# Slot stores and gathers tied to matmuls, and the experts' second layer kept two chunks behind

## The chip, the cores and the metric

The kernel runs on one core of one Trainium2 chip. The metric is the device time of one execution in microseconds (us), median of several runs. The engines are named as in the profile: PE is TensorE (matmuls), PEld its weight loads, DVE is VectorE, ACT is ScalarE, POOL is GpSimd, SP is SyncE, which here only issues DMAs. POOLq and the like are the engines' sequencers. "Idle before, releaser" is the time an engine stood idle before an instruction and what ended that; "issue" means that nothing which the profile shows was waited for.

## The reference, cut to what matters

2048 tokens of width 448 pass through two branches, and a gate per token mixes them:

```python
g = _sigmoid((x * gate_w).sum(-1, keepdims=True))
a = _A_ref(x, A_wqkv, A_w_phi, A_wo)      # linear attention, 16 heads of 28
b = _B_ref(x, B_w_gate, B_w1, B_w2)       # 8 experts, top 2 per token
return g * a + (1 - g) * b
```

Branch A: q, k, v from `x @ wqkv`; per head a 28x28 map, then two softmaxes (of the map and of its negative) joined to 56 features; `kv` is the sum over all tokens of features times v; each query's features are multiplied by it and normalised; then `@ wo`. Branch B: for each expert e, `h = silu(xf @ w1[e]) @ w2[e]` with 448 to 1792 to 448, weighted by the softmax over the two best logits, and zero for the other six experts.

## The kernel before, in words

Sums are made in pairs of a rounded high part and its remainder (`XH`, `XL` and so on), so one product is two or three matmuls; `kpairs` lists eleven pairs for a product over 448, and `mm3` issues them.

**Query, key and value tiles.** 16 tiles of 128 tokens. A first loop over them makes keys, values, logits and the running `kv` state. A second loop, `for t in range(NT + 2)`, is the one that the change touches first. Step t has, in the order of the program: `raise_` (exp on ScalarE, tile t + 3), `lower` (row maxima on VectorE, L562, and their subtraction on GpSimd, L563, tile t + 4), `attend(t)` (64 matmuls of 64x64 into two PSUM banks, L859) and `weigh(t)` (six VectorE operations, then an add and a copy on GpSimd that make `om`, L880 and L882), `project(t - 2)` (eleven matmuls, `ao`) with its output row stored by SP, `flip(t + 2)` (eight transposes, `et`), `turn(t - 1)` (four transposes of `om`, `ot`, L889), for the first nine steps `ask(t + 7)` (eleven matmuls), and then the GpSimd DMAs below.

**Routing.** `route` works out for each token its two experts, their weights and its slot in each expert's list, in two groups of eight tiles, a piece per step (`advance`). For each tile and choice one record per token is then written to a table in DRAM by an indirect DMA that GpSimd issues: `store(n)` takes the next n of the 32 (L455). Sixteen of them go in the first loop, between the loops and in step 0, sixteen in steps 2 to 6 (`STORES` gives the numbers that differ from 3). When all are issued, `table()` has SP read the lists back (sixteen small DMAs, L911), `rows(0, 1)` makes row numbers for expert 0 on GpSimd (L915, L919), `gather(0, c)` fetches the rows of chunk c of expert 0's tokens, 128 at a time (L768, five of them, two per step), `rows(1, E)` makes the other experts' numbers, and `first_tokens` turns the rows.

**Experts.** Experts are handled by size; the first has 552 places, the next two 544, the others 488 to 504. The hidden layer of 1792 is cut into 16 chunks (`fc`) of 128. Per chunk `first(e, fc, hf)` makes the first layer (`hp`, L115, in two pieces for the three large experts), silu on ScalarE (`hs`, L961) and its high and low part on VectorE (`hx`, L967 and L970). `second(e, fc)` adds the second layer into `acc` (L1021). Chunks whose first layer is issued wait in `held`; `keep` says how many may. Weights come two chunks at a time by SP (`wr`) and are split by ScalarE and VectorE (`halve`). At chunks 4 to 8 of expert e the rows of expert e + 1 are asked for, four indirect DMAs of 128 rows of 512 bytes per chunk of tokens (L772); at chunks 9 to 13 `tokens` has ScalarE copy (L783) and VectorE turn them. `leave(e)` weights the sums and adds them to the output by indirect DMAs of GpSimd (L934).

**What sets the order.** In both loops the order of TensorE, ScalarE and VectorE is that of the program. GpSimd and SP are ordered by a planner, but `in_turn` ties GpSimd's instructions of the loops to each other in the order of the program. `after(i, others)` makes an instruction wait for others by a semaphore, `follow` only keeps the order on one engine. The experts' gathers have no `in_turn`; they go as soon as one of the five `xg` buffers is free.

Of the kernel before, what the change touches and what calls it, by code (L numbers as in the profile page):

```python
# [18 lines left out]
P = 128  # L19
# [31 lines left out]
QASKS = {t: t + 7 for t in range(9)}  # L51
PEND = 0
ROWS = 1
SPLIT = 13
STORES = {3: 4, 4: 4, 5: 4, 6: 4}
VAHEAD = 6
AHEAD = 2
WARM = 2
# [16 lines left out]
def gated_mix(ctx: ExitStack, tc: tile.TileContext, xt, xq, wk, wq, wv, wphi, wo, w12, out):  # L75
# [13 lines left out]
    def after(i, others):  # L89
        for o in others:  # L90
            tc.add_manual_dep(i.ins, o.ins.name, mybir.DependencyInfo(mybir.DependencyClass.Sync,
                                                                      mybir.DependencyReason.DATA),
                              reason="what no_dep between its peers leaves out")

    def follow(i, o):
        tc.add_manual_dep(i.ins, o.ins.name, mybir.DependencyInfo(mybir.DependencyClass.NoSync,
                                                                  mybir.DependencyReason.SCHED_ONLY),
                          reason="what is needed sooner goes first")
# [4 lines left out]
    def in_turn(i, kind=None):  # L103
        if runs["on"]:
            if kind is None or kind != runs["kind"]:
                runs.update(before=runs["last"], last=[], kind=kind)
            for o in runs["before"]:
                follow(i, o)
            runs["last"].append(i)
        return i  # L110

    def mm3(o, pairs):
        n = len(pairs)
        for i, (a, b) in enumerate(pairs):
            nc.tensor.matmul(o, a, b, start=i == 0, stop=i == n - 1)  # L115

    def split(hi, lo, src, hi_engine="act"):
        if hi_engine == "act":
# [331 lines left out]
        nc.vector.tensor_copy(slot_i, slot_f)  # L450
        stores.extend((slot_i[:, t, k:k + 1], rec[:, ts.start + t, k, :]) for t in range(n) for k in range(2))

    def store(n):
        for at, what in stores[:n]:
            i = in_turn(nc.gpsimd.indirect_dma_start(  # L455
                out=tabd[:, :], out_offset=bass.IndirectOffsetOnAxis(ap=at, axis=0), in_=what, in_offset=None), "slots")
            after(i, filled)
            for o in sc:
                tc.declare_no_dep(i.ins, o.ins, reason="slots of their own")
            sc.append(i)  # L460
        del stores[:n]
# [87 lines left out]
    def signed(e):  # L549
        return e[:, :, 0:56].rearrange("p h (s d) -> p h s d", s=2)  # L550
# [5 lines left out]
        nc.scalar.activation(e4[:, :, 1], src, AF.Copy, scale=-1.0)  # L556


    def lower(e, n, pool):
        e4 = signed(e)  # L560
        mx = pool.tile([P, H, 2], F32, tag="mx", name=f"mx{n}", bufs=2)
        nc.vector.tensor_reduce(out=mx, in_=e4, axis=AX.X, op=ALU.max)  # L562
        in_turn(nc.gpsimd.tensor_tensor(out=e4, in0=e4, in1=mx.unsqueeze(3).to_broadcast([P, H, 2, DH]),  # L563
                                        op=ALU.subtract))


    def key(t):
# [178 lines left out]
    def extra(e):  # L746
        return EXS[e] if e < LARGE else 0
# [9 lines left out]
        return 4 if narrow(e) else 2  # L757


    def gather(e, c):  # L760
        if c == nm and not extra(e):
            return
        n = 4 if c < nm else -(-extra(e) // 32)
        t = pm.tile([P, 4, P], F32, tag="xg", name=f"xg{e}{c}", bufs=nm + 1)
        xg[e, c] = t
        if e == 0:
            ids, m = (idm[:, e * nm + c:e * nm + c + 1], P) if c < nm else (idx[:, e:e + 1], EX)
            in_turn(nc.gpsimd.indirect_dma_start(out=t[0:m].rearrange("p a k -> p (a k)"), out_offset=None, in_=x_rows,  # L768
                                                 in_offset=bass.IndirectOffsetOnAxis(ap=ids, axis=0)))
            return  # L770
        for b in range(n):
            i = nc.gpsimd.indirect_dma_start(  # L772
                out=t[:, b], out_offset=None, in_=xq,
                in_offset=bass.IndirectOffsetOnAxis(ap=idq[:, e, 4 * c + b:4 * c + b + 1], axis=0))
            if e == 1:
                for o in runs["last"]:
                    follow(i, o)


    def low_parts(pool, t, name, eng=nc.vector):  # L780
# [73 lines left out]
    def attend(t):  # L854
        n_ = two_banks(f"n{t}").rearrange("p (a j) (b d) -> p a (j b) d", a=2, b=2)
        for j in range(NJ):
            for a, h in enumerate(half):
                for b in half:
                    nc.tensor.matmul(n_[b, a, j, 0:60], et[t][h, j, b], B[h, j], start=True, stop=True)  # L859
        return n_.rearrange("p a j d -> p (a j) d")  # L860

    def weigh(t, n_):
# [39 lines left out]
    def table():  # L902
        for r in range(E):
            v = nc.values_load(byrank[0:1, r:r + 1], engines=SPONLY, min_val=0, max_val=E - 1)
            todo = [(tabm[:, r * nm:(r + 1) * nm], tabd[bass.ds(v * OWN, MAIN), :], P)]
            if r < LARGE:
                n = extra(r)
                for h in range(copies(r)):
                    todo.append((tabx[h * n:(h + 1) * n, r:r + 1], tabd[bass.ds(v * OWN + MAIN, n), :], n))
            for dst, src, p in todo:  # L910
                i = nc.sync.dma_start(dst, src.rearrange("(c p) two -> p c two", p=p))  # L911
                after(i, sc)
# [159 lines left out]
    for t in range(NT + 2):  # L1072
        u = t + QAHEAD
        if t - 1 in QASKS:
            signs(EQ[QASKS[t - 1]], pq[QASKS[t - 1]])
        elif t == 0:
            signs(EQ[6], pq[6])
        if 1 <= t and u - 1 < NT:
            raise_(u - 1)
        advance(QSTEPS.get(t, 2))  # L1080
        if u < NT and t < LOWER:
            lower(EQ[u], f"q{u}", pr)
        if t < NT:
            weigh(t, attend(t))
        if u < NT and t >= LOWER:
            lower(EQ[u], f"q{u}", pr)
        if t >= 2:
            if t == NT + 1:
                fill_in()
            leave_row(t - 2, project(t - 2))  # L1090
        if t + 2 < NT:
            flip(t + 2)
        if t == NT:
            fill_in()
        if 1 <= t <= NT:
            turn(t - 1)
        if t in QASKS:
            ask(QASKS[t], some=(0 if t else 5, 11))
        if t == NT - 1:
            fill_in()  # L1100
        if t == PEND:
            pe_stack.close()
            pm = ctx.enter_context(tc.tile_pool(name="pm", bufs=2, side="right", reuse_waits="tile"))
            pw = ctx.enter_context(tc.tile_pool(name="pw", bufs=1, side="right", reuse_waits="tile"))
            ph = ctx.enter_context(tc.tile_pool(name="ph", bufs=2, side="right", reuse_waits="tile"))
        store(STORES.get(t, 3))
        if at is None and not routes:
            routes.append(ranks())
            at = NT
        if at == NT and not stores and not routes:  # L1110
            table()
            at = t
        k = t - (NT if at is None else at)
        if k == ROWS:
            rows(0, 1)
        if k == ROWS + 3:
            rows(1, E)
        if ROWS <= k < ROWS + 3:
            for c in range(2 * (k - ROWS), min(2 * (k - ROWS) + 2, nm + 1)):
                gather(0, c)  # L1120
        if k == 2:
            load(0)
            splits += [halve(0, 1), halve(0, 2)]
        part_way()
        if ROWS + 2 <= k < ROWS + 3 + nm:
            g = first_tokens(k - ROWS - 2)
            next(g)
            coming.append(g)
        if SPLIT <= t < SPLIT + 3 and splits:
            if next(splits[0], 0) == 0:  # L1130
                del splits[0]
                if splits:
                    next(splits[0])
# [11 lines left out]
    for s in range(E * NFC):  # L1145
        e, fc = divmod(s, NFC)
        k, i = divmod(s, 2)
        token = tokens(e + 1, fc - 9) if e + 1 < E and 9 <= fc <= 9 + nm else iter(())
        next(token, 0)
        if i == 0 and k + 2 < E * NFC // 2:  # L1150
            load(k + 2)
        if k + 1 < E * NFC // 2:
            for _ in halve(k + 1, 1 + i):
                pass
        next(token, 0)
        if e + 1 < E and 4 <= fc <= 4 + nm:
            gather(e + 1, fc - 4)
        for hf in range(pieces(e)):
            if (e, fc, hf) not in fill:
                first(e, fc, hf)  # L1160
        held.append((e, fc))
        advance(1)
        if e == E - 1 and fc > NFC - LATE:
            continue

        keep = 1 if e == 0 or fc == 0 or fc >= 7 else 2
        while len(held) > keep:
            h = held.pop(0)
            second(*h)
            if h[1] == NFC - 1:  # L1170
                leave(h[0], order(h[0]))
                if h[0] == E - 2:
                    settle()
# [102 lines left out]
```

## Time and profile before

| what | value |
|---|---|
| median of 3 runs (lowest to highest) | 833.13 us (832.22 to 835.84) |
| the profiled execution: own time, span | 834.39 us, 832.7 us |
| mean granted TensorE clock | 0.988 |
| busy: PE, DVE, POOL, ACT | 804.8, 480.2, 342.4, 317.3 us |
| experts' gathers L772 | 114, 120.6 us of POOL |
| slot stores L455 | 32, 31.5 us of POOL |
| DMA, mean | 103 GB/s |

The second loop begins at about 117 us of the span and the experts' first chunk at about 228 us. In rows of instructions the columns are start, duration, engine, line, operation, output and inputs, count, and in brackets the idle time before it with its releaser. In rows of waits they are the total in us, the number of times, and the longest.

### The profile page before, as it was taken

The page shows a single profiled execution, that of the slowest core. Times are in us where ns is not written, and L with a number is a line of the kernel's source. Part 1 is how long each engine was busy: PE and PEld are TensorE (multiplying, and loading weights), DVE is VectorE, ACT ScalarE, POOL GpSimd, SP SyncE. Part 2 cuts the span into 40 slices and gives each one's busy share as a digit, 9 for nine tenths or more (in the row PEclk, how much of TensorE's full clock was granted, in tenths as well). Part 3 has the DMA queues.
Part 4 walks back from the last instruction along what each step waited for, and adds up shares of the span by engine and source line. Part 5 has one row for each costly group of instructions (what it writes and reads, how often), then busy time and mean ns, then how long its engine had stood idle before and what let it go on. Part 6 is the DMA issues. An engine that isn't in the chain of part 4 may idle for free. (4 is left out here: it accounts for less than half of the span.)

```text
span 832.7 us, 14729 instructions
## 1 busy us (share of the span) xinstructions
PE 804.8 (97%) x5672; PEld 712.7 (86%) x5672; DVE 480.2 (58%) x1048; ACT 317.3 (38%) x553; POOL 342.4 (41%) x344
## 2 busy tenths in 40 slices
PE   9999999899999899999999999999989999999996
PEld 6988887778999789998999888888878888888885
DVE  4597976456775567456645554654555465375431
ACT  5543454345642334333333342342433334244221
POOL 6666876665406256026614350730531143003003
PEclk9999998999999899999999999999999999999999
DMA  8420000015143226423733362463345237225303
GB/s 231 134 81 2 1 3 24 24 39 172 56 164 136 67 88 170 129 73 125 168 90 122 117 148 98 140 148 107 112 125 133 99 125 185 95 94 134 101 1 44
DMA packets 38910, 85.45 MB, mean 103 GB/s; under 512 B 11216, under 2 KB 19552, under 8 KB 38836
## 3 DMA queue, kind: packets, MB, share of 16 engines
q1 hardware_dynamic: 28612, 67.85, 24.6%
q0 software_dynamic: 10224, 16.61, 10.3%
q8 instruction: 46, 0.75, 0.4%
q14 instruction: 28, 0.23, 0.1%
HBM read 71.62 MB, written 12.82 MB: 101 GB/s over the span
## 5 line engine op out<-in xcount | busy, mean ns | idle before, releaser
L1021 PE MATMUL acc<-w2h,hx 128*128 128x448 f32 (+3 forms) x910 | 278.5, 367 | 3.2 <-DVE hx L967 3.1
L772 POOL DMA_INDIRECT xg<-in_xq_dram,idq x114 | 120.6, 1058 | 224.5 <-ACT xgh L799 172.0
L115 PE MATMUL hp<-xgh,w1h 128*128 128x272 f32 (+4 forms) x616 | 198.0, 336 | 5.7 <-ACT hs L961 3.1
L961 ACT ACTIVATE hs<-hp 128x272 f32<-128x272 f32 (+4 forms) x154 | 74.1, 484 | 323.7 <-issue 204.1
L115 PE MATMUL hp<-xgh,w1l 128*128 128x272 f32 (+4 forms) x616 | 196.9, 335 | 0.0
L1021 PEld LDWEIGHTS acc<-w2h,hx 128*128 128x128 f32 (+3 forms) x910 | 169.2, 186 | 26.3 <-issue 5.3
L967 DVE CAST hx<-hs 128x504 fp32r<-128x504 f32 (+5 forms) x154 | 56.2, 365 | 222.9 <-ACT hs L961 194.6
L1021 PE MATMUL acc<-w2l,hx 128*128 128x448 f32 (+1 forms) x462 | 169.4, 367 | 0.0
L115 PEld LDWEIGHTS hp<-xgh,w1h 128*128 128x128 f32 x616 | 116.3, 189 | 17.2 <-ACT hs L961 3.7
L115 PEld LDWEIGHTS hp<-xgh,w1l 128*128 128x128 f32 x616 | 116.4, 189 | 9.7
L934 POOL DMA_INDIRECT out_dram<-y,tabm x32 | 53.5, 1670 | 160.0 <-ACT y L1038 98.3
L115 PE MATMUL hp<-xgl,w1h 128*128 128x272 f32 (+4 forms) x462 | 104.4, 334 | 0.7 <-issue 0.7
L1021 PEld LDWEIGHTS acc<-w2l,hx 128*128 128x128 f32 (+1 forms) x462 | 85.9, 186 | 8.5
L970 DVE TENSOR_TENSOR hx<-hs,hx 128x276 fp32r<-128x276 f32 (+5 forms) x168 | 85.1, 514 | 5.3
L115 PEld LDWEIGHTS hp<-xgl,w1h 128*128 128x128 f32 x462 | 77.0, 189 | 8.8 <-issue 0.7
L741 DVE TENSOR_TENSOR w1l<-wr,w1h 128x1024 fp32r<-128x1024 f32 x56 | 68.0, 1215 | 3.6 <-ACT w1h L739 2.6
L741 DVE TENSOR_TENSOR w2l<-wr,w2h 128x896 fp32r<-128x896 f32 x56 | 60.3, 1076 | 11.0 <-ACT w2h L739 7.7
L739 ACT ACTIVATE w1h<-wr 128x1024 fp32r<-128x1024 f32 x56 | 58.9, 1052 | 0.0
L739 ACT ACTIVATE w2h<-wr 128x896 fp32r<-128x896 f32 x56 | 52.9, 945 | 0.0
L799 ACT ACTIVATE xgh<-xgt 128x512 fp32r<-128x512 f32 (+5 forms) x35 | 20.9, 597 | 38.1 <-DVE xgt L816 28.8
L586 POOL TENSOR_TENSOR ek<-ek,sk 128x896 f32<-128x896 f32 x16 | 27.1, 1699 | 19.0 <-DVE sk L585 9.1
L455 POOL DMA_INDIRECT tabd<-rec,slot_i x32 | 31.5, 984 | 7.6 <-issue 7.3
(221 smaller groups left out, 1020.8 us busy)
## 6 DMA issues: line engine op xcount, KB each, us to landing
wr<-in_w_dram SPq DMA_DIRECT2D x56, 512.0 KB
wr<-in_w_dram SPq DMA_DIRECT2D x56, 448.0 KB
xr<-in_xt_dram SPq DMA_DIRECT2D x15, 256.0 KB
out_dram<-aos SPq DMA_DIRECT2D x16, 224.0 KB
xg<-in_xq_dram,idq POOLq DMA_INDIRECT x114
out_dram<-zero SPq DMA_DIRECT2D x5, 224.0 KB
wraw_v<-in_wv_dram SPq DMA_DIRECT2D x4, 229.0 KB
wraw_k<-in_wk_dram SPq DMA_DIRECT2D x4, 224.0 KB
```

Source lines behind the costliest of these rows:

```text
L115: nc.tensor.matmul(o, a, b, start=i == 0, stop=i == n - 1)
L455: i = in_turn(nc.gpsimd.indirect_dma_start(out=tabd[:, :], out_offset=bass.IndirectOffsetOnAxis(ap=at, axis=0), in_=what, in_offset=None), ...
L586: in_turn(nc.gpsimd.tensor_tensor(out=by_head(e), in0=by_head(e), in1=s_.unsqueeze(2).to_broadcast([P, 2 * H, DH]), op=ALU.mult))
L739: nc.scalar.activation(h, raws[s][layer - 1], AF.Copy)
L741: nc.vector.tensor_tensor(out=l, in0=raws[s][layer - 1], in1=h.bitcast(F32), op=ALU.subtract)
L772: i = nc.gpsimd.indirect_dma_start(out=t[:, b], out_offset=None, in_=xq, in_offset=bass.IndirectOffsetOnAxis(ap=idq[:, e, 4 * c + b:4 * c ...
L799: nc.scalar.activation(xh, src, AF.Copy)
L934: return nc.gpsimd.indirect_dma_start(out=out, out_offset=bass.IndirectOffsetOnAxis(ap=idx_ap, axis=0), in_=y, in_offset=None, compute_op= ...
L961: nc.scalar.activation(hs[:, tsl], hp[:, 0:n], AF.Silu)
L967: nc.vector.tensor_copy(h[:, tsl], hs[:, tsl])
L970: nc.vector.tensor_tensor(out=h[:, a + o:b + o], in0=hs[:, a:b], in1=h[:, a:b].bitcast(F32), op=ALU.subtract)
L1021: nc.tensor.matmul(acc[e][c][:m, 0:D], l, r, start=fc == 0 and k == 0, stop=fc == NFC - 1 and k == len(pr) - 1)
```

## The change

In the second loop stores and expert 0's gathers move up to just behind `attend`, and each waits for the last matmul of `attend(t)`; the table's reading and `rows(0, 1)` move with them, and `rows(0, 1)` and the gathers of expert 0 come in the steps named below. Of `lower`, the maxima (`tops`) stay ahead of `attend`, and the subtraction (`drop`) comes behind the stores and gathers and ahead of `weigh`. The other experts' gathers become a generator that gives two DMAs per chunk from chunk 4 on, each waiting for the last matmul that `mm3` has issued, which is the last of the first layer of the chunk before. `keep` is 2 from chunk 1 to the last for experts 1 to 6, where it was 2 to chunk 6 only.

```diff
+ASKED = {1: (0, 1, 2), 2: (3, 4)}
-STORES = {3: 4, 4: 4, 5: 4, 6: 4}
+STORES = {6: 4}
...
-            nc.tensor.matmul(o, a, b, start=i == 0, stop=i == n - 1)
+            reached["pe"] = nc.tensor.matmul(o, a, b, start=i == 0, stop=i == n - 1)
...
-    def store(n):
+    def store(n, behind=()):
...
-            after(i, filled)
+            after(i, [*filled, *behind])
...
+    def gathers(e):
+        for c in range(nm + (extra(e) > 0)):
+            t = pm.tile([P, 4, P], F32, tag="xg", name=f"xg{e}{c}", bufs=nm + 1)
+            xg[e, c] = t
+            for b in range(4 if c < nm else -(-extra(e) // 32)):
+                i = nc.gpsimd.indirect_dma_start(
+                    out=t[:, b], out_offset=None, in_=xq,
+                    in_offset=bass.IndirectOffsetOnAxis(ap=idq[:, e, 4 * c + b:4 * c + b + 1], axis=0))
+                after(i, [reached["pe"]])
+                if e == 1:
+                    for o in runs["last"]:
+                        follow(i, o)
+                yield
...
-        if u < NT and t < LOWER:
-            lower(EQ[u], f"q{u}", pr)
+        early_top = u < NT and t < LOWER
+        if early_top:
+            top = tops(EQ[u], f"q{u}", pr)
         if t < NT:
-            weigh(t, attend(t))
-        if u < NT and t >= LOWER:
+            n_ = attend(t)
+        behind = [reached["n"]]
+        store(STORES.get(t, 3), behind)
+        if at is None and not routes:
+            routes.append(ranks())
+            at = NT
+        if at == NT and not stores and not routes:
+            table()
+            at = t
+        k = t - (NT if at is None else at)
+        if k == ROWS + 1:
+            rows(0, 1)
+        for c in ASKED.get(k - ROWS, ()):
+            gather(0, c, behind)
+        if early_top:
+            drop(EQ[u], top)
+        if t < NT:
+            weigh(t, n_)
+        if u < NT and not early_top:
             lower(EQ[u], f"q{u}", pr)
...
-        if k == ROWS:
-            rows(0, 1)
         if k == ROWS + 3:
             rows(1, E)
-        if ROWS <= k < ROWS + 3:
-            for c in range(2 * (k - ROWS), min(2 * (k - ROWS) + 2, nm + 1)):
-                gather(0, c)
...
-        if e + 1 < E and 4 <= fc <= 4 + nm:
-            gather(e + 1, fc - 4)
+        if e + 1 < E and fc == 4:
+            asked = gathers(e + 1)
+        if e + 1 < E and fc >= 4:
+            for _ in range(2):
+                next(asked, None)
...
-        keep = 1 if e == 0 or fc == 0 or fc >= 7 else 2
+        keep = 1 if e == 0 or fc == 0 or fc >= 7 and e == E - 1 else 2
```

More of the change, by code (lines that the diff above doesn't have):

```diff
@@ L110, in in_turn @@
         return i
+    reached = {}
     def mm3(o, pairs):
@@ L556, in signs, with tops, drop, lower @@
         nc.scalar.activation(e4[:, :, 1], src, AF.Copy, scale=-1.0)
-    def lower(e, n, pool):
+    def tops(e, n, pool):
+        mx = pool.tile([P, H, 2], F32, tag="mx", name=f"mx{n}", bufs=2)
+        nc.vector.tensor_reduce(out=mx, in_=signed(e), axis=AX.X, op=ALU.max)
+        return mx
+    def drop(e, mx):
         e4 = signed(e)
-        mx = pool.tile([P, H, 2], F32, tag="mx", name=f"mx{n}", bufs=2)
-        nc.vector.tensor_reduce(out=mx, in_=e4, axis=AX.X, op=ALU.max)
         in_turn(nc.gpsimd.tensor_tensor(out=e4, in0=e4, in1=mx.unsqueeze(3).to_broadcast([P, H, 2, DH]),
                                         op=ALU.subtract))
+    def lower(e, n, pool):
+        drop(e, tops(e, n, pool))
     def key(t):
@@ L757, in copies, with gather @@
         return 4 if narrow(e) else 2
[L760 to L763, printed above, removed]
+    def gather(e, c, behind):
         t = pm.tile([P, 4, P], F32, tag="xg", name=f"xg{e}{c}", bufs=nm + 1)
         xg[e, c] = t
[L766 to L777, printed above, removed]
+        ids, m = (idm[:, e * nm + c:e * nm + c + 1], P) if c < nm else (idx[:, e:e + 1], EX)
+        after(in_turn(nc.gpsimd.indirect_dma_start(out=t[0:m].rearrange("p a k -> p (a k)"), out_offset=None, in_=x_rows,
+                                                   in_offset=bass.IndirectOffsetOnAxis(ap=ids, axis=0))), behind)
+    def gathers(e):
[11 more added lines that the diff above has]
+                yield
     def low_parts(pool, t, name, eng=nc.vector):
@@ L858, in attend @@
                 for b in half:
-                    nc.tensor.matmul(n_[b, a, j, 0:60], et[t][h, j, b], B[h, j], start=True, stop=True)
+                    reached["n"] = nc.tensor.matmul(n_[b, a, j, 0:60], et[t][h, j, b], B[h, j], start=True, stop=True)
         return n_.rearrange("p a j d -> p (a j) d")
@@ L1105, in gated_mix @@
             ph = ctx.enter_context(tc.tile_pool(name="ph", bufs=2, side="right", reuse_waits="tile"))
[L1106 to L1113, printed above, removed]
-        if k == ROWS:
-            rows(0, 1)
         if k == ROWS + 3:
             rows(1, E)
-        if ROWS <= k < ROWS + 3:
-            for c in range(2 * (k - ROWS), min(2 * (k - ROWS) + 2, nm + 1)):
-                gather(0, c)
         if k == 2:
```

## The prediction

> **What bounds the kernel now.** I read the page first: how full TensorE is, and at which clock.
>
> ```profile
> span 832.7 us, 14729 instructions
> PE 804.8 (97%) x5672; PEld 712.7 (86%) x5672; DVE 480.2 (58%) x1048; ACT 317.3 (38%) x553; POOL 342.4 (41%) x344
> PEclk9999998999999899999999999999999999999999
> ```
>
> TensorE is busy for 97% of the span, so time can come only from its idle 28 us, from stretches at a lower clock, or from removed work; the change removes no matmul. So the next view is who TensorE waited for.
>
> ```profile
> PE n L859 <- issue: 8.7, 19, 1.1
> PE hp L115 <- issue: 3.3, 2, 2.7
> PE acc L1021 <- DVE hx L967: 3.1, 1, 3.1
> PE hp L115 <- ACT hs L961: 3.1, 3, 1.0
> ```
>
> The largest wait is inside attend (L859, 64 matmuls of 64x64 for one query tile), 19 times, on no semaphore that the profile shows ("issue"). The timeline of TensorE and GpSimd shows what runs then.
>
> ```profile
> 126.98 1.16 PE L859 MATMUL n<-B,et 64*64 64x60 f32 x64
> ...
> 134.08 1.06 PE L859 MATMUL n<-B,et 64*64 64x60 f32 x47
> 135.56 0.37 PE L859 MATMUL n<-B,et 64*64 64x60 f32 x5 [0.42 <-issue]
> ...
> 138.56 0.48 PE L859 MATMUL n<-B,et 64*64 64x60 f32 x3 [0.37 <-issue]
> ```
>
> ```profile
> 123.82 1.00 POOL L455 DMA_INDIRECT tabd<-rec,slot_i  x1 [0.16 <-issue]
> ...
> 134.25 1.00 POOL L455 DMA_INDIRECT tabd<-rec,slot_i  x1 [0.15 <-issue]
> ...
> 136.83 0.97 POOL L455 DMA_INDIRECT tabd<-rec,slot_i  x1 [0.30 <-issue]
> 137.82 1.72 POOL L563 TENSOR_TENSOR eq<-eq,mxq 128x896 f32<-128x896 f32 x1
> ...
> 143.34 0.99 POOL L455 DMA_INDIRECT tabd<-rec,slot_i  x1 [0.15 <-issue]
> ```
>
> Alone, attend takes 1.16 us (tile 2). In tile 3 three slot stores run beside it, 134.25 to 137.80: 47 of the 64 matmuls go, then a few at a time, and it lasts 4.96 us. The stall ends 0.8 us after the last store. So a store costs TensorE time only where it meets attend; beside the bigger matmuls it shows nothing (tile 4's four stores begin at 143.34, its attend only at 147.20). What each tile lost is in the table by stage, cut at the starts of attend (stretch, length, busy time of each engine, granted clock, DMA share and GB/s).
>
> ```profile
> 134.08:147.20 13.12, 11.24 (x99) 9.43 (x99) 5.66 (x17) 4.02 (x7) 8.99 (x10) 0.74 0.06 19
> 147.20:155.62 8.42, 7.38 (x99) 6.57 (x98) 4.41 (x10) 3.91 (x7) 5.35 (x6) 1.00 0.10 30
> 155.62:167.70 12.08, 9.75 (x99) 8.37 (x98) 4.16 (x10) 4.03 (x7) 8.23 (x9) 0.86 0.07 20
> 167.70:176.66 8.96, 7.88 (x100) 6.70 (x99) 3.98 (x10) 4.02 (x7) 5.43 (x6) 1.00 0.09 29
> 176.66:183.75 7.09, 7.09 (x99) 6.34 (x98) 4.29 (x10) 3.92 (x7) 4.37 (x6) 1.00 0.16 4
> 183.75:192.28 8.53, 7.66 (x100) 6.74 (x99) 4.12 (x10) 3.91 (x7) 5.62 (x7) 1.00 0.65 147
> 192.28:197.81 5.53, 5.17 (x89) 4.61 (x88) 2.86 (x7) 3.02 (x6) 3.29 (x3) 1.00 0.94 328
> 197.81:203.80 5.99, 5.39 (x88) 4.68 (x87) 4.13 (x9) 3.07 (x7) 2.65 (x5) 1.00 0.35 130
> 203.80:209.07 5.27, 5.27 (x92) 4.82 (x92) 4.04 (x9) 3.63 (x8) 4.34 (x8) 1.00 0.15 55
> ```
>
> The rows are tiles 3 to 11. Tile 7 (7.09 us, TensorE full) is the undisturbed period with an ask, tile 11 (5.27 us) without one. Tiles 3 and 5 also ran at a clock of 0.74 and 0.86, behind their idle stretches; the page's clock row shows the dip.
>
> In the experts the other three waits stand at the end of long runs of gathers.
>
> ```profile
> 252.26 1.06 POOL L772 DMA_INDIRECT xg<-in_xq_dram,idq  x1 [21.12 <-DVE idq L925]
> ...
> 274.27 0.94 POOL L772 DMA_INDIRECT xg<-in_xq_dram,idq  x1 [0.30 <-issue]
> ...
> 609.23 0.94 POOL L772 DMA_INDIRECT xg<-in_xq_dram,idq  x1 [0.30 <-issue]
> ```
>
> ```profile
> 306.88 0.39 PE L115 MATMUL hp<-xgh,w1h 128*128 128x276 f32 x1 [0.96 <-ACT hs L961]
> ...
> 384.38 0.39 PE L115 MATMUL hp<-xgh,w1h 128*128 128x272 f32 x1 [1.05 <-ACT hs L961]
> ...
> 462.45 0.39 PE L115 MATMUL hp<-xgh,w1h 128*128 128x272 f32 x1 [1.05 <-ACT hs L961]
> ```
>
> ```profile
> 264.38:270.02 5.64, 5.64 (x37) 5.39 (x36) 0.77 (x3) 0.40 (x1) 4.42 (x5) 1.00 0.60 221
> 270.02:281.81 11.79, 8.46 (x37) 7.68 (x36) 5.52 (x16) 2.98 (x5) 3.98 (x5) 0.71 0.09 28
> 602.09:607.04 4.95, 4.95 (x24) 4.29 (x23) 3.68 (x9) 1.88 (x4) 3.58 (x4) 1.00 0.24 60
> 607.04:615.70 8.66, 5.49 (x24) 4.14 (x23) 3.25 (x6) 2.86 (x4) 2.52 (x3) 1.00 0.36 134
> ```
>
> Seventeen gathers run back to back from 252.26 to 275.2, and one chunk of expert 0 takes 11.79 us instead of 5.64; at the end of a run that stops at 610.2, a chunk takes 8.66 instead of 4.95. I read both places as one thing: something that TensorE's instructions fill empties slowly while GpSimd issues indirect DMAs. Attend fills it with 64 short matmuls in a microsecond; chunks fill it only over some 20 us of gathers.
>
> **The change, part by part.** *Stores and expert 0's gathers behind attend.* Sixteen stores of tiles 2 to 6 (3, 3, 3, 3, 4) and five gathers (tiles 8 and 9) now start after their tile's attend. Three stores take 3.55 us (134.25 to 137.80), and each further one 1.29 (134.25 to 136.83 for two), so four take 4.8. From the end of one attend to the start of the next an undisturbed tile leaves 7.09 - 1.16 = 5.93 us, and the stall's tail was 0.8: even four stores end just in time (4.8 + 0.15 + 0.8 = 5.75). What goes: against 7.09, tiles 3 to 6 and 8 lose 6.03, 1.33, 4.99, 1.87 and 1.44 us; against 5.27, tiles 9 and 10 lose 0.26 and 0.72. Sum 16.6 us. The two stores ahead of tile 0's attend stay.
>
> *What now stands behind the stores* on GpSimd: drop (the subtract of L563, 1.72 us) and the om add with its copy.
>
> ```profile
> 141.75 1.14 POOL L880 TENSOR_TENSOR om<-w 128x448 f32<-128x448 f32 x1 [2.22 <-DVE w L875]
> 142.95 0.24 POOL L882 COPY om<-om 128x64 f32<-128x64 f32 x1
> 180.96 0.60 PE L889 MATMUL ot<-ident,om 128*128 128x128 f32 x4
> ```
>
> Add and copy take 1.45 us, so om is ready 0.15 + 3.55 + 1.72 + 1.45 = 6.9 us after attend, 8.2 with four stores. It is used by the ot transposes of the next tile, 4.3 us after that attend's start (176.66 to 180.96), which is 5.93 + 4.3 = 10.2 us after its own attend: 2 us of cover. Without the cover the excess would be paid once per store tile. The raise on ScalarE waits for drop, 5.4 to 6.7 us after attend, when the next tile begins; its next user is a flip one tile on. Both cost nothing. The table's 16 small DMAs on SP follow the last store as before, ahead of weigh instead of behind turn; output rows queue behind them in both versions. rows(0,1) moves from tile 7 to 8, half a microsecond of GpSimd ahead of three gathers: 4.4 us, inside the same 5.93; the tiles that read them come in tile 9, behind drop and om. Nothing.
>
> *Residue.* The trace has no case of several stores just behind an attend. Nearest is the one store at 123.82, after which nothing stalls: 0. From the other side, tile 3's stalled rate (17 matmuls in 3.9 us) over 3.6 us of stores passes 16 matmuls, which otherwise need about 2.8 us (34 in 5.93): 0.8 us lost in each of seven tiles, 5.6. A gain here has no source, as the losses are already taken out whole. I take 1.5, nearer the row that was seen.
>
> *Experts' gathers, two per chunk behind the previous chunk's first layer.* Two take 2.5 us of a chunk of 4.95 to 5.64, and the rest of the chunk drains. So the runs of 12 to 17 disappear: 11.79 - 5.64 = 6.15, 8.66 - 4.95 = 3.71, and 0.96 + 1.05 + 1.05 = 3.06: 12.9 us. Queued behind a waiting gather are only scatter-adds of the expert before, whose rows nobody reads until the next one's. Tokens of chunk 3 are used at chunk 12, with their last gather issued at chunk 11: 2.5 us to issue, and landing. A landing is sized by the last store, for which SP waited:
>
> ```profile
> 175.05 0.99 POOL L455 DMA_INDIRECT tabd<-rec,slot_i  x1 [0.15 <-issue]
> ...
> 177.30 0.42 SPq L911 DMA_DIRECT2D tabm<-tabd  x1
> ```
>
> That is 1.3 us behind its end at 176.04; 2.5 + 1.3 = 3.8 of 4.95. Hidden, and a further chunk of cover stands behind it.
>
> *Second layer two chunks behind from chunk 7 on* (experts 1 to 6). It moves no matmul: the two seconds in one step go from chunk 7 to the next chunk 0. Chunks 1 to 6 run so already, with no other wait in the list above: 0. If the longer-held w2 or hx buffers bound, it would be a fraction of a chunk per expert.
>
> **Sum.** 834.4 (this execution's own time) - 16.6 - 12.9 + 1.5 = 806.4. The median shown, 833.1, lies 1.3 lower, so between 805 and 806.4; I say 806.
>
> **Rivals.** (a) Only the query tiles gain: two gathers per chunk are enough to keep the backlog. 834.4 - 16.6 + 1.5 = 819. Against it: the first 19 us of the long run cost nothing. Or only the experts gain, because the stall follows the stores to the transposes: about 821. Together 0.14.
>
> (b) The stalls belong to the recording and the timed runs lack them. Then the timed runs stay at 833. The recorded execution and the median of the timed ones differ by 1.3 us where the stalls cost 29.5, so I give this 0.06. [...]
>
> (c) Slower: late gathers. ScalarE copies gathered rows ahead of the chunk's silu, so a gather that lands after its chunk holds up silu and then TensorE. Price: (landing - 2.45 - 4.95) per expert, seven times. To get past 838 it needs 4.6 us each, so a landing of 12 us against 1.3 seen. Against it: the chunks above have DMA shares of 0.09 to 0.60. 0.04, with 840.
>
> **How the numbers follow.** Forecast 0.74 (803 to 812, the residue's ends); (a) 0.14; (b) 0.06; (c) 0.04; 0.02 for no change by some other way. The range 802 to 822 holds the forecast and (a). Half a percent, 4.2 us, is about what a measurement tells from no change: faster 0.88, same 0.08, slower 0.04.
>
> **What would show it.** Right: attend at 1.16 us in tiles 3 to 10, each store's start just behind it, the "issue" wait of L859 under 2 us, no clock under 1.00 between 134 and 200, gathers in pairs one chunk apart, no chunk of 8 us but those with two second layers. Wrong: "issue" waits at the et or ot transposes (residue), ot waiting for om, or silu waiting for the copy of a gather.

## Result, and the profile after

On the occasion of the prediction the changed kernel took 804.46 us (median of 6 runs, 803.56 to 804.98) against 833.49 us for the kernel before (6 runs, 832.22 to 840.20): ratio 0.9637 [0.9605, 0.9669]. The profiled execution took 804.68 us, with a span of 803.0. The forecast was 806. Two things must be said at once, since the numbers below can't be read without them. The records of that occasion don't name its chip. The experiments ran later on two named chips, and on one of them the kernel before takes 802.9 us, not 833.

The page of the changed kernel, the same three lines:

```profile
span 803.0 us, 14733 instructions
PE 790.7 (98%) x5672; PEld 703.5 (88%) x5672; DVE 482.5 (60%) x1048; ACT 318.9 (40%) x553; POOL 344.6 (43%) x344
PEclk9999999999999999999999999999999999999999
```

The span fell by 29.7 us. TensorE's idle time fell from 27.9 to 12.3, so 15.6 of it; the other 14.1 came off its busy time for the same 5672 matmuls. The granted clock, 0.988 before and 0.998 now, is some 8 of that, an estimate from these two (1% of 800): behind the longest stalls the clock was lower too (0.74 and 0.86 in the prediction's rows of tiles 3 and 5, 0.71 in the long chunk of expert 0), and in the trace before most `ao` matmuls took 0.57 us from 139.0 to 143.0 us, at a clock of 0.50, against 0.36 at a clock of 1.00 in tile 7. Most of the rest is the stalled attends themselves, whose pieces count as busy: those of tiles 3 to 6 and 8 to 10 add up to 13.8 us before, where seven times 1.16 is 8.1. The clock row has no dip left.

Who TensorE waited for (total us, times, longest):

```profile
PE n L870 <- issue: 2.1, 3, 1.0
PE warm L204 <- DVE zero L202: 1.5, 1, 1.5
PE pv L313 <- ACT WHv L122: 0.7, 1, 0.7
PE n L870 <- DVE w L886: 0.2, 1, 0.2
```

That is the whole list: no wait of the experts (`hp`, `acc`) is left, and the attend wait (now L870) fell from 8.7 to 2.1 us. The three that remain, in TensorE's timeline:

```profile
118.65 0.61 PE L870 MATMUL n<-B,et 64*64 64x60 f32 x22 [0.55 <-issue]
...
133.86 1.16 PE L870 MATMUL n<-B,et 64*64 64x60 f32 x64
...
163.63 0.64 PE L870 MATMUL n<-B,et 64*64 64x60 f32 x26 [0.60 <-issue]
...
188.74 0.61 PE L870 MATMUL n<-B,et 64*64 64x60 f32 x25 [0.97 <-issue]
```

The first is tile 0, whose stores were left ahead of it. Tiles 3 to 6 are like 133.86: 64 matmuls in 1.16 us. The second is tile 7: the last of tile 6's four stores, 161.71 to 162.68, runs on beside its first 0.44 us. The third, tile 11, is new and has no GpSimd DMA beside it. The table by stage, cut at the starts of attend in tiles 3, 7, 9, 10 and 11 (columns as before the change), shows what stood there instead:

```profile
133.86:140.96 7.10, 7.10 (x100) 6.34 (x99) 6.62 (x16) 3.92 (x7) 5.95 (x7) 1.00 0.11 35
...
162.24:170.21 7.97, 7.37 (x100) 6.58 (x99) 4.27 (x10) 4.03 (x7) 6.98 (x9) 1.00 0.10 4
...
177.30:182.13 4.83, 4.83 (x88) 4.38 (x88) 3.38 (x8) 3.02 (x6) 3.95 (x6) 1.00 0.92 249
182.13:186.96 4.83, 4.83 (x88) 4.39 (x87) 3.63 (x9) 3.19 (x7) 3.38 (x5) 1.00 0.98 325
186.96:193.46 6.50, 5.53 (x92) 4.94 (x91) 4.56 (x10) 3.63 (x8) 5.34 (x10) 1.00 0.33 119
```

Tile 11 comes behind 9.7 us in which the weight loads kept the DMA engines at 0.92 and 0.98. Tiles 9 and 10 took 4.83 us, less than the 5.27 taken as their undisturbed period: that row has 92 matmuls and theirs 88, for it holds four transposes of expert 0's tokens that they don't have.

GpSimd's timeline in tiles 2 to 4: `om` copy, three stores (two shown), `drop`, `om` add and copy, next store; and the last store of tile 6.

```profile
135.60 0.26 POOL L893 COPY om<-om 128x64 f32<-128x64 f32 x1
136.32 0.99 POOL L458 DMA_INDIRECT tabd<-rec,slot_i  x1 [0.46 <-issue]
...
138.90 0.96 POOL L458 DMA_INDIRECT tabd<-rec,slot_i  x1 [0.30 <-issue]
139.87 1.73 POOL L569 TENSOR_TENSOR eq<-eq,mxq 128x896 f32<-128x896 f32 x1
141.53 1.17 POOL L891 TENSOR_TENSOR om<-w 128x448 f32<-128x448 f32 x1
142.77 0.24 POOL L893 COPY om<-om 128x64 f32<-128x64 f32 x1
143.49 0.99 POOL L458 DMA_INDIRECT tabd<-rec,slot_i  x1 [0.48 <-issue]
...
161.71 0.97 POOL L458 DMA_INDIRECT tabd<-rec,slot_i  x1 [0.31 <-issue]
```

The store at 136.32 comes 1.30 us after attend(3) ended (133.86 + 1.16 = 135.02), and its bracket does not name attend: it follows the `om` copy of the tile before. GpSimd does one tile in 143.49 - 136.32 = 7.17 us, a little more than TensorE's 7.09, so the stores come later from tile to tile: 1.30, 1.37, 1.45 and 1.54 us behind attend in tiles 3 to 6. In tile 6, with four stores, that is too late, and the last one meets attend 7.

In the experts the gathers now go in pairs, each pair released by a first layer:

```profile
246.34 0.95 POOL L781 DMA_INDIRECT xg<-in_xq_dram,idq  x1 [2.70 <-PE hp L118]
247.59 0.95 POOL L781 DMA_INDIRECT xg<-in_xq_dram,idq  x1 [0.30 <-issue]
251.99 0.95 POOL L781 DMA_INDIRECT xg<-in_xq_dram,idq  x1 [3.45 <-PE hp L118]
```

Where the gain lies, by two milestones, the first layer of expert 0 and the first scatter of its output, in the kernel before and then the one after:

```profile
227.84 0.37 PE L115 MATMUL hp<-xgh,w1h 128*128 128x276 f32 x1
...
321.94 1.51 POOL L934 DMA_INDIRECT out_dram<-y,tabx  x1 [5.06 <-DVE y L1040]
```

```profile
212.22 0.38 PE L118 MATMUL hp<-xgh,w1h 128*128 128x276 f32 x1
...
298.88 1.51 POOL L945 DMA_INDIRECT out_dram<-y,tabx  x1 [17.80 <-DVE y L1051]
```

Query tiles 227.84 - 212.22 = 15.62 us; expert 0 another 23.06 - 15.62 = 7.44; the other seven experts 29.7 - 23.06 = 6.64.

### The profile page after: what moved, and what is told of

It is laid out like the page before. It is cut to its first block, busy times and chain, and to the rows that moved or that the text cites. A ratio compares the mean times of both kernels' runs of the same rounds, so it can differ in the third digit from the quotient of the medians.

```text
span 803.0 us, 14733 instructions
## 1 busy us (share of the span) xinstructions
PE 790.7 (98%) x5672; PEld 703.5 (88%) x5672; DVE 482.5 (60%) x1048; ACT 318.9 (40%) x553; POOL 344.6 (43%) x344
## 5 line engine op out<-in xcount | busy, mean ns | idle before, releaser
L781 POOL DMA_INDIRECT xg<-in_xq_dram,idq x114 | 122.7, 1076 | 175.2 <-PE hp L118 134.7
L945 POOL DMA_INDIRECT out_dram<-y,tabx x10 | 15.0, 1500 | 67.6 <-DVE y L1051 60.3
```

The costliest lines, as they stand in the source:

```text
L781: i = nc.gpsimd.indirect_dma_start(out=t[:, b], out_offset=None, in_=xq, in_offset=bass.IndirectOffsetOnAxis(ap=idq[:, e, 4 * c + b:4 * c ...
L945: return nc.gpsimd.indirect_dma_start(out=out, out_offset=bass.IndirectOffsetOnAxis(ap=idx_ap, axis=0), in_=y, in_offset=None, compute_op= ...
```

## The experiments

The theory in them: GpSimd's indirect DMAs hold TensorE up where they meet attend's short matmuls (4.96 us instead of 1.16 in the prediction's trace), or run for 20 us beside chunks (11.79 instead of 5.64). The rivals: only one half of the change gains; the new order gains and not the waits; any DMA does it.

**One half at a time, four kernels.** `e_query_only` is the kernel after with the experts' gathers free to start, four per chunk, and the old `keep`; `e_gathers_only` the kernel before with the generator of gathers alone; `e_keep_only` the kernel before with the new `keep` alone; `e_old_keep` the kernel after with the old one.

```diff
# e_query_only, on the kernel after
-                after(i, [reached["pe"]])
-            for _ in range(2):
+            for _ in range(4):
-        keep = 1 if e == 0 or fc == 0 or fc >= 7 and e == E - 1 else 2
+        keep = 1 if e == 0 or fc == 0 or fc >= 7 else 2
# e_gathers_only, on the kernel before (the generator itself, as in the change, left out)
...
-        if e + 1 < E and 4 <= fc <= 4 + nm:
-            gather(e + 1, fc - 4)
+        if e + 1 < E and fc == 4:
+            asked = gathers(e + 1)
+        if e + 1 < E and fc >= 4:
+            for _ in range(2):
+                next(asked, None)
# e_keep_only, on the kernel before
-        keep = 1 if e == 0 or fc == 0 or fc >= 7 else 2
+        keep = 1 if e == 0 or fc == 0 or fc >= 7 and e == E - 1 else 2
# e_old_keep, on the kernel after
-        keep = 1 if e == 0 or fc == 0 or fc >= 7 and e == E - 1 else 2
+        keep = 1 if e == 0 or fc == 0 or fc >= 7 else 2
```

> The changed kernel with its query tiles as they are, but the experts' gathers four per chunk without a wait and the second layer as before. Theory (stalls come where indirect DMAs of GpSimd meet attend, or run on for some 20 us; the wait and place of the DMAs cure both; the second layer's lag is worth nothing): the query tiles' 15 us stay and the experts' 14 us are lost again, 818 us. Rival (the lag of the second layer brings the experts' part): 818 as well. Rival (only one common cause, so that one part cures all): 805 or 833.

> The kernel before with only the experts' gathers changed (two per chunk, each behind the previous chunk's first layer); second layer and query tiles as before. Theory: 833.5 - 14 = 819.5 us, no idle stretch of 1 us or more in the experts. Rival (the second layer's lag brings it): 833.

> The kernel before with only the second layer two chunks behind to the end of experts 1 to 6. Theory: nothing for the whole runs of gathers; at most the waits for a late silu or hx in experts 1 to 6 (1.05, 1.05 and 3.7 us) get cover from the extra chunk, so 828 to 834 us. Rival (the lag brings the experts' part): 819.5.

> The changed kernel with the old lag of the second layer (one chunk from chunk 7 on). Theory: 804.5 us, no difference that can be measured, since no silu is late once the gathers come in pairs. Rival (the lag is needed): 808 to 818, with waits of acc for hx from chunk 7 on.

Measured on chip 10, against a kernel before of 802.93 us (31 runs, 801.98 to 803.62), ten runs each:

| kernel | median us | ratio |
|---|---|---|
| e_query_only | 802.57 | 0.9996 [0.9987, 1.0006] |
| e_gathers_only | 802.78 | 1.0000 [0.9990, 1.0010] |
| e_keep_only | 802.75 | 0.9999 [0.9989, 1.0008] |
| e_old_keep | 802.74 | 0.9997 [0.9988, 1.0007] |

The four expectations started from 833 us, and none of the times that they set against each other could come out. On this chip the second layer's lag is worth nothing, in either kernel; but no silu is late here, so what it is worth where they are late was not tried. The halves can't be told apart here, because the thing they were to take away is absent. `e_keep_only` has the queries of the kernel before, unchanged. TensorE and then GpSimd in its tiles 3 and 4 (attends 5 and 6 take 1.16 us too, but without the stalls the stores no longer meet them, but for 0.2 us of attend 5):

```profile
133.99 1.20 PE L859 MATMUL n<-B,et 64*64 64x60 f32 x64
141.13 1.16 PE L859 MATMUL n<-B,et 64*64 64x60 f32 x64
```

```profile
134.21 1.00 POOL L455 DMA_INDIRECT tabd<-rec,slot_i  x1 [0.15 <-issue]
135.51 0.97 POOL L455 DMA_INDIRECT tabd<-rec,slot_i  x1 [0.30 <-issue]
136.79 0.97 POOL L455 DMA_INDIRECT tabd<-rec,slot_i  x1 [0.30 <-DVE z L870]
141.06 0.99 POOL L455 DMA_INDIRECT tabd<-rec,slot_i  x1 [0.15 <-issue]
```

Three stores start at 134.21, as near to attend as the 134.25 of the kernel before, and attend takes 1.20 us, where the prediction's trace had 4.96. At 141.06 a store begins that runs beside attend(4) for all but its last 0.24 us: 1.16. The same instructions in the same places, without the stall.

Loading of instructions, a rival that the prediction didn't name, doesn't fit. The DMA view counts the same 46 and 28 packets of kind "instruction" in the trace before, in the kernel after and in `x_before_heavy` below, where attend's "issue" waits sum to 8.7, 2.1 and 7.5 us, and in the trace before none of them stands between 140 and 150 us, where attend 4 stalls for 1.04 us.

**Is it the wait or the order, and do long runs cost?** `e_order_no_wait` keeps the new order without the wait for attend; `e_one_run` lets all gathers of an expert go at chunk 4, behind one wait.

```diff
# e_order_no_wait
-        behind = [reached["n"]]
+        behind = []
# e_one_run
-            for _ in range(2):
+            for _ in range(20):
                 next(asked, None)
```

> The changed kernel with the stores and expert 0's gathers in their new place in GpSimd's order, but without the wait for attend. The trace after shows that in tiles 3 to 6 the stores start 0.46 us after the om copy of the tile before and 1.2 to 1.5 us after their attend, so the wait was over before GpSimd got there. Theory A (the place in the order does it; the wait binds only where GpSimd is idle, in tile 0 and at the gathers of tile 8): 806 us, attend at 1.16 us in tiles 3 to 6, stalls of 1 to 2 us in tile 8 and perhaps in tile 2 or 3. Theory B (the wait does it): 819 us, stalls in tiles 3 to 6 as before the change.

> The changed kernel with all 16 or 17 gathers of an expert let go at once at chunk 4, still behind a matmul, so that they run back to back for 20 us. Theory (a long run of gathers fills something): several us lost per expert, as in the long runs before (6.2 us in expert 0, 3.7 in a run of 16 in a later one), 0.5 to 1 where the extra chunk of lag covers it; 811 to 825 us in all, every loss near the end of a run or just behind it. Rival (the early start of the gathers cost the time, by meeting something else at that place): 804.5.

On chip 10 again, with the kernel before at 802.69 us (22 runs): 802.55 us, 1.0000 [0.9990, 1.0009], and 802.64 us, 1.0001 [0.9992, 1.0010]. In `e_one_run` seventeen gathers go back to back from 234.80 to 258.94 us, as long a run as the one that cost a chunk 6.15 us in the prediction's trace. TensorE's waits there:

```profile
PE warm L204 <- DVE zero L202: 1.5, 1, 1.5
PE pv L313 <- ACT WHv L122: 1.2, 1, 1.2
PE n L870 <- DVE w L886: 0.6, 1, 0.6
```

No chunk waits for anything. Neither the waits nor the pairs have a price or a worth in time on this chip, so neither theory of the two runs was decided for the occasion with stalls.

The trace of `e_order_no_wait` does show what the wait changes. Without it GpSimd stands idle 0.15 to 0.16 us ahead of a tile's first store, with it 0.46 to 0.48, and a tile of three stores takes it 6.8 us instead of 7.17. That is less than TensorE's 7.09, so the stores creep up on attend: in tile 6 the first begins at 155.44, inside attend(6), 154.57 to 155.73. The place in the order alone does not keep them apart; the wait does, and its 0.3 us per tile is part of why the fourth store of tile 6 came late in the kernel after.

**The stall of tile 0 taken away.** `v_first_stores` moves the two stores between the loops behind attend 0, where a third already stood, and runs routing earlier, so that two of tile 6's four stores go behind attend 1. It was to remove the 0.55 and 0.60 us that were left.

```diff
-QSTEPS = {0: 1, 1: 1}
+QSTEPS = {0: 2, 1: 2}
-TSTORES = 2
+TSTORES = 0
-STORES = {6: 4}
+STORES = {1: 2, 6: 2}
```

> The changed kernel with two edits meant to take away two of its remaining stalls: no stores between the loops (all three that are left of the first group go behind attend of tile 0) and the second group routed one step earlier, so that tile 1 takes two stores and tile 6 two instead of four. Theory: the stalls of 0.55 us in tile 0 and 0.60 in tile 7 go, 803.3 us, which five rounds may just not tell from 804.5. Rival (the routing on VectorE delays weigh and attend of tile 1): 804.5 or 1 more.

On chip 10: 807.12 us (6 runs), 0.6% slower than the kernel before (ratio 1.0059 [1.0047, 1.0071]). The two stalls are absent on this chip anyway (attends 0 and 7 take 1.16 us in `e_old_keep`), so only the price shows. Tiles 0 and 1 are short ones (4.8 us each in the kernel after), and here the price that the prediction named shows itself: `om` queued behind stores. TensorE, and the VectorE operation that ran ahead of both waits:

```profile
125.44 0.66 PE L900 MATMUL ot<-ident,om 128*128 128x128 f32 x4 [1.59 <-POOL om L891]
130.03 1.16 PE L870 MATMUL n<-B,et 64*64 64x60 f32 x64 [1.70 <-DVE w L886]
```

```profile
122.03 3.45 DVE L451 TENSOR_TENSOR s<-sel,slot 128x64 f32<-128x64 f32 x1
125.76 0.23 DVE L451 TENSOR_TENSOR s<-sel,slot 128x64 f32<-128x64 f32 x1
```

The same operation takes 0.23 us once and 3.45 us while GpSimd works through a store, `drop` and the `om` add (121.60 to 125.38). The second wait is for `w`, which VectorE makes behind it.

**Which DMAs stall TensorE, if any?** Four kernels put extra DMAs behind attends 12 and 13 of the kernel after, so that they meet the next attends: five indirect stores of GpSimd each (`x_pool`), five plain DMAs of GpSimd (`x_pooldirect`), ten small ones of SP (`x_sp`), four copies of 960 KB by SP (`x_heavy`). Nothing is left out.

```diff
# x_heavy; the others differ in the DMA and in the number, 5, 5 and 10
+    def probe(t, behind):
+        for k in range(4):
+            n = len(probes)
+            i = nc.sync.dma_start(spare[n * P:(n + 1) * P, :], w12[40 + n, :, :])
+            after(i, behind)
+            probes.append(i)
...
+        if t in PROBED:
+            probe(t, behind)
         if early_top:
             drop(EQ[u], top)
```

> The changed kernel with five additional record stores to an unused table issued by GpSimd behind attend of tile 12 and five behind attend of tile 13, where nothing stalled. They take 6.4 us of 5.27, so they run on beside the next attend. Theory 1 (GpSimd's issuing of indirect DMAs starves attend): attend of tiles 13 and 14 takes 2 to 5 us instead of 1.16, nothing in the other matmuls. Theory 2 (any DMA traffic does it): the same here; it is told apart by the next runs. Theory 3 (the stall belonged to the place, tiles 3 to 10): 1.16 us.

> As the run with five additional indirect stores per tile behind attend of tiles 12 and 13, but as plain DMAs of GpSimd (same records, rows given by address). Theory 1 (GpSimd's issuing): stalls in attend of tiles 13 and 14 if they last until it, 1 to 5 us each. Theory 1b (only the indirect form): 1.16 us.

> As the run with five additional indirect stores per tile, but ten plain DMAs of the same records per tile issued by SP, some 6 us of issuing. Theory 1 (GpSimd's issuing): attend stays at 1.16 us in tiles 13 and 14. Theory 2 (small writes to DRAM, whoever issues them): stalls of 1 to 5 us as with GpSimd.

> The changed kernel with four DRAM-to-DRAM copies of 960 KB behind attend of tile 12 and four behind tile 13, issued by SP, so that the DMA engines are busy throughout tiles 13 to 15 with no GpSimd DMA. The trace after has one stall of 0.97 us in tile 11's attend with no GpSimd DMA near it and the DMA engines full. Theory 1 (GpSimd's issuing alone): attend stays at 1.16 us in tiles 13 to 15. Theory 2 (full DMA engines do it too): stalls of 0.5 to 2 us in some of these.

One run each on chip 10, the kernel before at 802.34: 810.9, 802.56, 803.97 and 808.68 us. In `x_pool` attends 13 and 14 took 1.19 and 1.16 us beside the stores; its time went elsewhere, in a wait that pays for `om` behind stores a second time (total, times, longest):

```profile
PE ot L917 <- POOL om L893: 3.8, 2, 3.5
```

The plain and the small DMAs left attends 13 and 14 at 1.16, though the plain ones ended 0.5 us after attend 13 began and 0.2 us after attend 14 did, and so hardly met them. Since beside stores attend took at most 1.20 us in the traces of this chip, these runs can't say which DMAs do where stalls exist. The traces of chip 10 hold two "issue" stalls in attend, and neither has a GpSimd DMA beside it. One is of 0.30 us at attend 11 of `x_pool` (185.26 to 186.97), ahead of the first extra store (193.80). The other is behind the copies. Attends 13 to 15 in `x_heavy`, and the table by stage of the first two and the start of the third:

```profile
196.39 1.16 PE L872 MATMUL n<-B,et 64*64 64x60 f32 x64
201.66 1.16 PE L872 MATMUL n<-B,et 64*64 64x60 f32 x64
206.09 1.15 PE L872 MATMUL n<-B,et 64*64 64x60 f32 x61
208.79 0.33 PE L872 MATMUL n<-B,et 64*64 64x60 f32 x3 [1.55 <-issue]
```

```profile
196.39:201.66 5.27, 5.27 (x92) 4.82 (x91) 3.52 (x9) 2.73 (x7) 2.24 (x5) 1.00 1.05 373
201.66:206.09 4.43, 4.43 (x85) 3.98 (x84) 3.52 (x9) 2.82 (x6) 1.40 (x5) 1.00 1.11 385
206.09:211.00 4.91, 3.35 (x73) 3.00 (x73) 4.28 (x10) 1.65 (x3) 1.92 (x3) 0.93 1.00 330
```

After 9.7 us at DMA shares of 1.05 and 1.11 attend stalls once, near its end, for 1.55 us, as tile 11 of the kernel after did for 0.97 behind 9.7 us at 0.92 and 0.98. So these two stalls had no GpSimd DMA beside them. That suggested, as a guess, a condition from outside: a memory path that was loaded on the first occasion.

**The kernel before under load.** `x_before_heavy` tests that.

```diff
+PROBED = {2: 3, 3: 2, 4: 2, 5: 2, 6: 2}
...
-            weigh(t, attend(t))
+            n_ = attend(t)
+            probe(PROBED.get(t, 0), [reached["n"]])
+            weigh(t, n_)
```

> The kernel before, with eleven extra copies of 960 KB from DRAM to DRAM issued by SP, three behind attend 2 and two behind each of attends 3 to 6, so that the DMA engines are nearly full (share above 0.9, where it was about 0.1) while the slot stores of steps 2 to 6 run beside attends 3 to 7. Nothing of the computation is left out. Theory (the stall needs the stores and a loaded DMA or memory path, which the first occasion had from outside and this one lacks): attends 3 to 6 stall again, 2 to 4 us each for those with stores beside them, an issue wait of 6 to 15 us in all, time 810 to 820. Rival 1 (full DMA engines alone do it, stores add nothing): one or two stalls of 1 to 1.6 us as beside the copies of the kernel after, time 804 to 809, stalls as often at attend 7, which has no store beside it, as at 3 to 6. Rival 2 (neither does it): attends 3 to 7 stay at 1.16 to 1.20, and what is lost, 0 to 6 us, stands in waits for the table's reading or the output rows.

This one ran on another chip, chip 2, 13 minutes after the last: 829.78 us, and the unchanged kernel before beside it 831.53, one run each. TensorE's waits in `x_before_heavy`, its attends 3 and 7, and the table by stage of the same two (start to just behind the end):

```profile
PE n L870 <- issue: 7.5, 15, 1.1
PE hp L116 <- issue: 2.2, 4, 1.1
PE hp L116 <- ACT hs L972: 1.7, 2, 0.9
```

```profile
133.82 1.08 PE L870 MATMUL n<-B,et 64*64 64x60 f32 x48
...
137.49 0.34 PE L870 MATMUL n<-B,et 64*64 64x60 f32 x4 [0.39 <-issue]
...
175.87 1.16 PE L870 MATMUL n<-B,et 64*64 64x60 f32 x64
```

```profile
133.80:138.00 4.20, 2.62 (x66) 1.98 (x66) 2.11 (x6) 1.82 (x3) 3.41 (x5) 1.00 0.74 257
...
175.80:177.10 1.30, 1.30 (x66) 1.16 (x66) 0.78 (x2) 1.06 (x3) 0.36 (x1) 1.00 0.13 47
```

The stalls that the theory expected came, at a time that none of the three expected, and not for the theory's reason: the kernel before without any copies is as slow on this chip (831.53 us against 829.78). Attend 3 lasts 137.83 - 133.82 = 4.01 us at a DMA share of 0.74, against 4.96 at a share of 0.06 over that tile in the prediction's trace, and the attend waits sum to 7.5 against 8.7, so the copies didn't lengthen them either. Attend 7, which has no store beside it, takes 1.16, as before; since the copies had ended by then (0.13), load alone was not tried on this chip. Attend 8, also behind the copies, has two gathers beside it (183.39 to 185.77) and stalls again, 182.97 to 186.63; its tile takes 11.16 us, where tile 7 took 7.10. The experts' waits on "issue" and on `hs` are back as well (2.2 and 1.7 us at `hp`).

What the runs show, then: with the same code in the query tiles the stalls are there on one chip and not on another. The kernel before takes 831.5 to 833.5 us where they are and 802.3 to 802.9 where they are not (medians of three sets, 54 runs). Its own trace is from the first occasion, whose chip has no name: on chip 2 the stalls are seen in `x_before_heavy`, and the unchanged kernel's time says that they were there without the copies. The changed kernel takes 804.5 where they are. On chip 10 it was not timed itself; its nearest relative, `e_old_keep`, differs by the lag alone and takes 802.74.

## Why the prediction was right, and where it was not

**The query tiles.** Forecast 16.6 less 1.5 of residue, 15.1; measured 15.62. The residue came in other coin than the one named: 0.88 us at tile 7 (7.97 against 7.09) and 1.23 at tile 11 (6.50 against 5.27), where nothing was expected; tiles 9 and 10 gave 0.44 each beyond what was counted, since they were measured against a row with four transposes more. 16.6 - 2.11 + 0.88 = 15.4, and another 0.23 lies ahead of tile 0's attend (117.20 against 117.43). That the sum came within 0.5 us is luck in part: the 1.5 had no row of its own, and a loss of 2.11 that nobody expected was offset by an uncounted gain of 0.88.

**The experts.** Forecast 6.15 and 0.96 in expert 0, 7.1; measured 7.44. Forecast 3.71 and two times 1.05 behind it, 5.8; measured 6.64. Rival (a), that only one half gains, is excluded on that occasion by these two milestones. They don't part the pairs from the second layer's lag, which changed together.

**Stores 0.15 us behind attend.** Wrong: 1.30, because GpSimd was still at the `om` of the tile before. The step added up what follows the stores and did not ask when GpSimd comes to them; a tile's list is 7.17 us long. With that, `om(3)` was ready at 143.01, 7.99 us after its attend and not 6.9. The deadline of 10.2 us was right, so this cost nothing: `ot` waited for `om` nowhere in the kernel after. What it did cost is the step "even four stores end just in time": the four of tile 6 began 1.54 us behind attend, and with 4.8 of their own they ended 6.4 us behind it, where 5.93 were free. That overlap is where tile 7 stalled and lost 0.88 us. `v_first_stores` and `x_pool` show the price where the cover is gone, as the prediction said it would be paid.

**The second layer's lag: nothing.** It is nothing on chip 10, by `e_keep_only` and `e_old_keep`. Whether part of the 6.64 us is the lag's, as cover for a late silu, no run shows.

**Late gathers, rival (c).** TensorE waited for no silu in the kernel after; right.

**What failed** is the sentence "something that TensorE's instructions fill empties slowly while GpSimd issues indirect DMAs", as a property of the kernel; it was the author's reading, and no run shows what would fill or empty. The coincidence of stores and stalls was read rightly, and chip 2 shows it again: attends 3 to 6 with stores and 8 with gathers stall, 7 without does not. But the stores are not sufficient. On chip 10 the same stores at the same distance cost attend at most 0.04 us. The trace of one execution could not have told this, and no rival in the prediction named it.

**The argument against rival (b)** was probably void, though the rival itself failed in the timed runs, which fell by 29 us. Every timed run here comes with a span and a clock of its own, so all seem to have been recorded; if so, that the recorded execution agreed with the median says nothing on a run without recording. In the traces before and after, 38 to 55 matmuls of attend pass beside GpSimd's DMAs ahead of the first stop, and then, in tiles 3, 5, 6, 8 and 10 of the trace before, a few at a time. No run here shows what stops them, or an execution without records.

**Open:** what differs between the chips, or between the occasions, for the chip and the occasion changed together and chip 2 was seen once; whether the stalls need the recording; how much of the experts' gain is the lag's; whether the place in the order would have done without the wait where stalls exist; and what busy DMA engines and the indirect DMAs have in common, as attend stopped behind DMA shares of 0.92 to 1.11 (0.97 and 1.55 us) and beside the stores at 0.06 (tile 3 of the trace before). That the changed kernel gains on chip 2 was not tried.

## What to carry to other kernels

The idle gaps whose releaser is "issue", 8.7 us of attend here, had a cause that the profile did not show; before a change is built on such a gap, look at the same kernel's trace from a second chip, for the gap may not be there, as on chip 10. Short matmuls in a burst are where the stall landed first here (attend, 4.96 us instead of 1.16 beside three stores), so keeping GpSimd's indirect DMAs off them is cheap insurance where GpSimd's order allows it: the whole change, gathers of the experts and lag included, was worth 29 us where the stall exists, and its nearest relative nothing where it doesn't. When work is put ahead of something on an engine, add up that engine's whole period first, and ask when it comes to the work: `om` behind stores was free in periods of 7.09 us and cost 1.6 to 3.5 us in the shorter ones, and a list of 7.17 us in a period of 7.09 ran late until a store met the next attend.

## What the runs showed of the hardware that was not expected

- One kernel, two times: 802.3 to 802.9 us on chip 10, 831.53 on chip 2 some 13 minutes later (one run).
- 64 matmuls of 64x64 beside three indirect stores: 1.20 us on chip 10 (`e_keep_only`), 4.01 on chip 2 (`x_before_heavy`), there with copies at a DMA share of 0.74 as well (4.96 without, on the occasion of the prediction).
- The same burst stopped with no GpSimd DMA beside it: for 1.55 us in `x_heavy` behind DMA shares of 1.05 and 1.11, for 0.97 at tile 11 of the kernel after behind 0.92 and 0.98, and for 0.30 at tile 11 of `x_pool`.
- A VectorE operation on 128x64 took 3.45 us instead of 0.23 beside a store, `drop` and the `om` add of GpSimd (`v_first_stores`).
- Five plain DMAs of GpSimd took 2.82 us together (`x_pooldirect`); five indirect ones 6.17 (193.80 to 199.97, `x_pool`).
